# A windowed attention and gMLP kernel on one core: a new order of all steps, other engines for copies, and another choice of gMLP steps in 64-column halves

## The chip, the core and the metric

The kernel runs on one core of a Trainium2 chip. A core has five engines, each with its own queue of instructions that it takes strictly in order: TensorE (PE, matrix products), VectorE (DVE), ScalarE (ACT), GpSimd (POOL) and SyncE (SP, which issues nearly all DMAs here; its steps are marked DQ). Engines wait for one another by semaphores. The metric is device time of one execution in microseconds (us); lower is better.

## What is computed

Sliding-window attention (8 batches, 8 heads, 576 positions, head size 64, window 64), then a gMLP layer with a spatial gate over its output:

```python
scores = scale * np.matmul(q, k.transpose(0, 1, 3, 2))
mask = (rel >= 0) & (rel < window)
scores = np.where(mask, scores, -1000000000.0)
attn = np.exp(scores - max); attn = attn / (sum(attn) + 1e-09)
x = attn @ v                                # to (batch, 576, 512)
h = np.maximum(x @ w_in, 0.0)               # 512 -> 1024
u, v = h[..., :512], h[..., 512:]
v_n = (v - mu) / np.sqrt(var + 1e-06)
v_s = np.einsum('ts,bsd->btd', w_spatial, v_n) + b_spatial[None, :, None]
out = (u * v_s) @ w_out                     # 512 -> 512
```

## The kernel before

The program is 1113 steps. Each is a small function that emits the instructions of one piece of work for one engine. A step's name gives its kind, batch and part. Lines are those of kernel.py.

Loading, for batch b and group g of four heads (`load_steps`, line 419): `ldq`, `ldk` (line 424, 128x1152 f32 each) and five `ldv` (line 445, 128 rows of v each, the last 64; cut in packets of 256 bytes) are DMAs. `cq`, `ck` cast to f16; `tq`, `tk` (line 431) transpose on DVE. `cv` casts v into `hv`; `sl`, `su` and `s4` copy it into `hs`, shifted by 64 rows. On POOL a cast of q or k is three instructions (`cp`, line 314), on ACT or DVE one. Which engine does a copy is not fixed in the function: the listed step says it.

Attention (`att_steps`, 478, and `rem_steps`, 547, for the last 64 queries, marked `_r`): S is the scores (64 small matmuls in tiles of 32 rows, line 490), E the exponential on ACT (497), M the mask as a minimum on DVE (500), Z the sums (513), N and n logarithm and exponential of minus it, so the inverse, on ACT (539, 541), P the product with v (524), X the scaled result on DVE (532).

gMLP (`gmlp_steps`, 669), per batch: V_0 to V_3 (679) and V_4 (691; it also does the last 64 output rows of the batch before, 694) give the v half; Vr (658, ACT) takes it out of PSUM, Vb and Va (660, 662, DVE) make mean and variance, L1 and L2 (ACT) the inverse deviation, A (717, DVE) the normalized rows. U_0 to U_4 and Ur (746, ACT) give the u half. G multiplies by the spatial matrix, Ge (776, DVE) gates. O and Oe (635, ACT) give the output, `st` stores it. At the start `ldwin`, `ldwsp`, `ldwo`, `ldb` load the weights in pieces, `cwin`, `cwsp`, `cwo`, `cb` cast them, and W0 to W4 with We0 to We4 transpose the spatial matrix. D steps are filler matmuls on a zero tile.

What sets the order: the string `ORDER` (line 18) lists every step with its engine and the buffer numbers that it takes. `as_listed` (183) reads it, and lines 828 to 836 emit the steps in that order. So each engine's queue is the list cut down to its steps, and a load waits in SP's queue until the earlier user of its buffer (`BUFS`, 150: 8 for q, k and weights, 4 for v) is done with it. PSUM has two pairs of banks for S and four single banks (0 to 3) for all other products; a product waits until the bank's earlier content has been taken out.

`halves` (606) emits a product of a gMLP step. A step in the set `HALVED` does each product as two matmuls with 64 columns of weights into the two halves of the partitions (line 611) instead of one with 128 columns (line 608). Z, P, V_4 and O7_4 always work in 64 columns, S always in 32-row tiles. Before, `halved(2)` (197) chooses by rule: a run of gMLP products goes in halves where 64-column steps stand on both sides of it, or on one side of a run of at most two; U0_0 to U0_4 are added. That gives 92 steps in halves.

Of the kernel before, what the change touches and what calls it, by code (L numbers as in the profile page):

```python
# [26 lines left out]
ldwin110:DQ:7 cv0_01:DVE N0_00:ACT:2 ldwin111:DQ su0_01:DVE sl0_01:POOL Z0_r:PE:2 su0_10:DVE
Z0_11:PE:3 ldwin101:DQ N0_r:ACT:3 D9:PE:0 s40_0:POOL tk1_0:DVE:5 n0_00:ACT ldb:DQ:1 D8:PE:1
ldk1_1:DQ:2 n0_10:ACT D13:PE:2 ldq1_1:DQ:3 n0_01:ACT P0_01:PE:0 cv0_11:DVE ldwin000:DQ:0 P0_00:PE:1
sl0_11:DVE su0_11:POOL N0_11:ACT:4 S1_0:PE:0:1 ldwin001:DQ X0_00:DVE:0 ldwin010:DQ:4 n0_11:ACT  # L30
cwin110:POOL D20:PE:2 s40_1:DVE ldwin011:DQ E1_00:ACT:1 D19:PE:3 cwin111:POOL X0_01:DVE P0_10:PE:1
ldwsp3:DQ:5 P0_11:PE:2 cwin101:POOL E1_01:ACT:0 X0_10:DVE:1 D18:PE:3 ldwsp2:DQ:7 D3:PE:0 X0_11:DVE
cwin100:ACT P0_r:PE:1 M1_00:DVE n0_r:ACT cb:ACT V0_1:PE:3 ldwsp1:DQ:6 M1_01:DVE ck1_1:POOL:2
V0_2:PE:0 X0_r:DVE:0 Vr0_1:ACT:0 ldwsp4:DQ:1 Z1_00:PE:2 Vb0_1:DVE:0 V0_0:PE:1 N1_00:ACT:5
ldv1_00:DQ:2 cq1_1:POOL:3 tk1_1:DVE:0 Vr0_2:ACT:1 V0_3:PE:3 Vr0_0:ACT:2 cwin000:ACT ldwsp0:DQ:2
n1_00:ACT Z1_01:PE:2 V0_4:PE:0 D25:PE:1 D26:PE:1 ldv1_01:DQ cwin010:POOL tq1_1:DVE:1 cwin001:ACT
N1_01:ACT:2 cwin011:POOL ldv1_02:DQ Vr0_3:ACT:3 Vb0_2:DVE:1 S1_1:PE:0:1 cwsp3:POOL ldv1_03:DQ
Vr0_4:ACT:4 Vb0_0:DVE:2 U0_2:PE:1 E1_11:ACT:2 cwsp2:POOL Vb0_3:DVE:3 U0_3:PE:2 Va0_2:DVE cwsp1:POOL
E1_10:ACT:3 Va0_3:DVE Va0_1:DVE Vb0_4:DVE:4 U0_4:PE:3 Va0_0:DVE Va0_4:DVE M1_11:DVE ldv1_04:DQ
L10:ACT:0 U0_1:PE:0 Ur0_3:ACT:0 M1_10:DVE ldk2_0:DQ:3 Ur0_2:ACT:1 S1_r:PE:1:0 ldv1_10:DQ:3 cwsp4:DVE  # L40
Z1_11:PE:2 L20:ACT Ur0_1:ACT:2 U0_0:PE:1 A0_4:DVE cwsp0:DVE E1_r0:ACT:1 ldv1_11:DQ E1_r1:ACT
A0_0:DVE:0 Ur0_4:ACT:3 W0:PE:0 A0_3:DVE:1 ldq2_0:DQ:0 N1_11:ACT:1 cv1_00:DVE:2 cv1_01:POOL W2:PE:3
ldv1_12:DQ M1_r:DVE Ur0_0:ACT:4 W3:PE:2 ldv1_13:DQ sl1_00:ACT:2 sl1_01:POOL W4:PE:1 We0:DVE
s41_0:ACT We2:DVE We3:ACT W1:PE:0 su1_01:POOL su1_00:DVE Z1_r:PE:3 We4:ACT ldv1_14:DQ ck2_0:POOL:0
A0_2:DVE:2 P1_01:PE:2 N1_r:ACT:0 P1_00:PE:1 ldk2_1:DQ:4 Z1_10:PE:3 A0_1:DVE:3 ldwo10:DQ:5 We1:DVE
N1_10:ACT:4 ldq2_1:DQ:7 X1_00:DVE:2 G0_4:PE:0 n1_01:ACT ldwo00:DQ:6 G0_3:PE:3 n1_10:ACT ldwo11:DQ
cv1_10:POOL:3 X1_01:DVE ldwo01:DQ tk2_0:DVE:2 sl1_10:ACT:3 su1_10:POOL G0_0:PE:1 cq2_0:ACT:1
ldq3_0:DQ:1 cv1_11:POOL ldv2_00:DQ:0 Ge0_3:DVE:0 s41_1:POOL G0_2:PE:2 sl1_11:ACT Ge0_4:DVE:1
su1_11:POOL n1_r:ACT tq2_0:DVE:3 n1_11:ACT ldk3_0:DQ:2 G0_1:PE:3 ck2_1:POOL:2 cwo10:ACT ldv2_01:DQ
Ge0_2:DVE:2 P1_10:PE:0 P1_11:PE:2 X1_10:DVE:3 S2_0:PE:1:0 X1_11:DVE cq2_1:POOL:3 ldv2_02:DQ  # L50
P1_r:PE:0 E2_00:ACT:0 Ge0_0:DVE:3 U1_2:PE:2 ldv2_03:DQ Ge0_1:DVE:4 E2_01:ACT:1 U1_1:PE:1 X1_r:DVE:1
M2_00:DVE Ur1_2:ACT:5 V1_3:PE:3 cwo01:POOL tk2_1:DVE:0 cwo11:ACT Ur1_1:ACT:0 cwo00:POOL V1_1:PE:0
Vr1_3:ACT:5 M2_01:DVE cq3_0:POOL:0 V1_2:PE:2 Vr1_1:ACT:6 ldv2_10:DQ:1 Vb1_3:DVE:5 V1_4:PE:1
ldv2_11:DQ tq2_1:DVE:1 Vr1_2:ACT:7 Z2_01:PE:3 Vr1_4:ACT:4 V1_0:PE:0 ck3_0:POOL:1 Vb1_2:DVE:1
N2_01:ACT:3 tq3_0:DVE:4 S2_1:PE:1:0 Oe0_4:ACT:0 ldv2_12:DQ Vr1_0:ACT:2 U1_0:PE:2 ldk3_1:DQ:3
cv2_00:POOL:1 Va1_2:DVE E2_11:ACT:3 Va1_3:DVE ldv2_13:DQ Vb1_1:DVE:3 Z2_00:PE:3 O0_2:PE:1 ldv2_14:DQ
Vb1_0:DVE:0 E2_10:ACT:2 Vb1_4:DVE:2 ldv2_04:DQ U1_4:PE:0 N2_00:ACT:5 Va1_1:DVE ldv3_10:DQ:2
S2_r:PE:0:1 Va1_0:DVE Va1_4:DVE tk3_0:DVE:5 L11:ACT:1 O0_0:PE:3 Oe0_2:ACT:0 ldq3_1:DQ:0 E2_r0:ACT:0
ldv3_11:DQ Ur1_4:ACT:3 M2_11:DVE U1_3:PE:1 L21:ACT ldv3_12:DQ E2_r1:ACT A1_4:DVE Oe0_0:ACT:1
O0_1:PE:0 A1_2:DVE:4 ldq4_0:DQ:4 Ur1_0:ACT:1 A1_3:DVE:5 ldv3_13:DQ A1_1:DVE:6 Ur1_3:ACT:4  # L60
S3_0:PE:0:1 A1_0:DVE:7 ldv5_10:DQ:3 n2_00:ACT M2_10:DVE Z2_11:PE:3 Oe0_1:ACT G1_0:PE:2 M2_r:DVE
sl2_00:ACT:0 su2_00:POOL Z2_r:PE:1 N2_11:ACT:2 G1_3:PE:0 Ge1_0:DVE:5 s42_0:ACT cv2_10:POOL:0
# [120 lines left out]
def as_listed(plan):  # L183

    by = {s.name: s for s in plan.steps}
    out = []
# [10 lines left out]
def halved(longest):  # L197
# [6 lines left out]
    for name in seq:  # L204
        if not runs or runs[-1][0] != kind(name):
            runs.append((kind(name), []))
# [660 lines left out]
```

## Time and profile before

| what | value |
|---|---|
| time, median of 3 runs | 199.65 us (199.64 to 199.7) |
| profiled execution, span from first to last instruction | 198.2 us |
| its own whole time | not listed; the median is 1.4 us over its span |
| PE busy | 187.3 us (94%), 3337 matmuls |
| ACT busy | 168.4 us (85%) |
| DVE busy | 158.4 us (80%) |
| POOL busy | 76.9 us (39%) |
| DMA moved | 42.74 MB, mean 216 GB/s |
| granted TensorE clock | 0.998 |

Busy time is the union of an engine's instructions; matmuls overlap, so PE's is no sum of its steps. Windows give the same numbers for a stretch of the span, with the share of time in which the 16 DMA engines had packets (it can exceed 1, as packets overlap). The chain of waits is followed back from the last instruction; its rows are start, length and what held the end up. "DMA to landing" is the time from a load's issue to the last of its packets.

### The profile page before, as it was taken

The page shows a single profiled execution, that of the slowest core. Times are in us where ns is not written, and L with a number is a line of the kernel's source. Part 1 is how long each engine was busy: PE and PEld are TensorE (multiplying, and loading weights), DVE is VectorE, ACT ScalarE, POOL GpSimd, SP SyncE. Part 2 cuts the span into 40 slices and gives each one's busy share as a digit, 9 for nine tenths or more (in the row PEclk, how much of TensorE's full clock was granted, in tenths as well). Part 3 has the DMA queues.
Part 4 walks back from the last instruction along what each step waited for, and adds up shares of the span by engine and source line. Part 5 has one row for each costly group of instructions (what it writes and reads, how often), then busy time and mean ns, then how long its engine had stood idle before and what let it go on. Part 6 is the DMA issues. An engine that isn't in the chain of part 4 may idle for free.

```text
span 198.2 us, 7839 instructions
## 1 busy us (share of the span) xinstructions
PE 187.3 (94%) x3337; PEld 109.7 (55%) x3337; DVE 158.4 (80%) x306; ACT 168.4 (85%) x305; POOL 76.9 (39%) x147
## 2 busy tenths in 40 slices
PE   7788999999999999989999999999999999999991
PEld 2333565666556665565476567466465565764450
DVE  4799999999796899869999798887958684757420
ACT  2589889878899999989999999999999999558341
POOL 5232584747776689121999299100000000000000
PEclk9999999999999999999999999999999999999999
DMA  6998999999689989989999993878721110500535
GB/s 221 384 289 178 383 365 222 308 366 372 140 203 286 343 239 255 276 195 266 322 253 235 262 294 83 251 205 228 235 107 65 49 41 5 215 0 0 179 115 187
DMA packets 50278, 42.74 MB, mean 216 GB/s; under 512 B 39361, under 2 KB 39489, under 8 KB 50242
## 3 DMA queue, kind: packets, MB, share of 16 engines
q1 hardware_dynamic: 50018, 41.91, 71.9%
q8 instruction: 26, 0.43, 0.9%
q10 hardware_dynamic: 224, 0.33, 0.5%
q14 instruction: 10, 0.08, 0.1%
HBM read 32.79 MB, written 9.44 MB: 213 GB/s over the span
## 4 chain that ended last, share of the span: by engine, by line
PE 42%; ACT 20%; DMA 20%; DVE 6%; SPq 5%; issue 3%; POOL 3%; POOLq 0%
PE bank L611 17%; PE bank L608 17%; DMA nv<-in_v_dram 9%; DMA nk<-in_k_dram 7%; SPq L445 4%; DMA ws<-in_moe_w_spatial_dram 4%; ACT e L497 3%; ACT ob L635 3%; ACT lz L539 3%; ACT hs L316 2%; ACT lz L541 2%; PE pair L490 2%; PE bank L524 2%; ACT ru L746 2%; ACT vs L658 2%
## 5 line engine op out<-in xcount | busy, mean ns | idle before, releaser
L497 ACT ACTIVATE e<-pair 128x1024 f16<-128x1024 f32 x32 | 31.8, 1024 | 2.8 <-PE pair L490 2.6
L611 PE MATMUL bank<-wspT,vn 128*64 128x512 f16 (+3 forms) x440 | 32.4, 296 | 0.3
L776 DVE TENSOR_TENSOR g<-bank,ru 128x512 f16<-128x512 f32 (+1 forms) x40 | 24.6, 629 | 9.1 <-PE bank L608 4.4
L660 DVE BATCH_NORM_STATS2 st<-vs 128x6 f32<-128x512 f16 (+1 forms) x40 | 25.7, 671 | 2.8 <-ACT vs L658 2.8
L658 ACT ACTIVATE vs<-bank 128x512 f16<-128x512 f32 (+1 forms) x40 | 23.0, 602 | 5.6 <-PE bank L611 3.2
L532 DVE TENSOR_TENSOR x<-bank,lz 128x512 f16<-128x512 f32 x32 | 21.4, 683 | 6.5 <-PE bank L524 5.0
L746 ACT ACTIVATE ru<-bank 128x512 f32<-128x512 f32 (+1 forms) x40 | 21.6, 562 | 4.5 <-PE bank L608 4.4
L635 ACT COPY ob<-bank 128x512 f32<-128x512 f32 (+1 forms) x39 | 22.8, 589 | 2.1 <-PE bank L608 1.9
L611 PEld LDWEIGHTS <-vn 128*64 128x64 f16 (+1 forms) x440 | 18.6, 110 | 10.7 <-issue 1.3
L319 POOL CAST hk<-nk 128x384 f16<-128x384 f32 x33 | 16.3, 530 | 19.3 <-DMA nk<-in_k_dram 18.9
L500 DVE TENSOR_TENSOR e<-e,mask 128x1024 f16<-128x1024 f16 x32 | 21.9, 701 | 1.2 <-ACT e L497 1.2
L611 PE MATMUL bank<-win,x 128*64 128x512 f16 x184 | 22.4, 379 | 0.0
L431 DVE STREAM_TRANSPOSE qT<-hq 128x576 f32<-128x576 f32 x16 | 19.8, 1240 | 3.2 <-POOL hq L319 3.0
L611 PE MATMUL bank<-x,win 128*64 128x512 f16 (+1 forms) x288 | 22.3, 298 | 0.0
L431 DVE STREAM_TRANSPOSE kT<-hk 128x576 f32<-128x576 f32 x16 | 19.9, 1246 | 0.7 <-POOL hk L319 0.4
L541 ACT ACTIVATE lz<-lz 128x512 f32<-128x512 f32 x32 | 19.7, 635 | 0.1
L539 ACT ACTIVATE lz<-bank 128x512 f32<-128x512 f32 x32 | 18.6, 606 | 1.2 <-PE bank L513 1.1
L717 DVE TENSOR_SCALAR vn<-vs,mv,ln 128x512 f16<-128x512 f16 (+1 forms) x40 | 15.8, 447 | 4.2 <-ACT ln L707 4.1
L319 POOL CAST hq<-nq 128x384 f16<-128x384 f32 x30 | 15.7, 559 | 7.4 <-DMA nq<-in_q_dram 6.4
L322 POOL COPY hs<-hv 64x512 f16<-64x512 f16 (+1 forms) x28 | 16.2, 607 | 4.4 <-issue 3.7
L816 PE MATMUL bank<-scratch 128*128 128x512 f16 (+1 forms) x68 | 15.6, 379 | 1.3 <-DVE scratch L257 1.3
L611 PE MATMUL bank<-wout,g 128*64 128x512 f16 x128 | 16.1, 380 | 0.0
(89 smaller groups left out, 333.0 us busy)
## 6 DMA issues: line engine op xcount, KB each, us to landing
nq<-in_q_dram SPq DMA_DIRECT2D x16, 576.0 KB, 6.0
nk<-in_k_dram SPq DMA_DIRECT2D x16, 576.0 KB, 5.8
nv<-in_v_dram SPq DMA_DIRECT2D x64, 128.0 KB, 5.2
out_dram<-ob SPq DMA_DIRECT2D x14, 512.0 KB, 4.7
wi<-in_moe_w_in_dram SPq DMA_DIRECT2D x8, 256.0 KB, 6.0
ws<-in_moe_w_spatial_dram SPq DMA_DIRECT2D x4, 288.0 KB, 7.0
nv<-in_v_dram SPq DMA_DIRECT2D x16, 64.0 KB, 4.8
wo<-in_moe_w_out_dram SPq DMA_DIRECT2D x4, 256.0 KB, 8.1
```

The lines of the kernel that those rows point to most:

```text
L319: nc.gpsimd.tensor_copy(o[:, n:n + 384], i[:, n:n + 384])
L431: d = add(f"t{name}{b}_{g}", ("DVE", 1.09), key, lambda e: nc.vector.transpose(qt.t[:, :].rearrange("p (i j) -> p j i", j=18), h.t[:, :].b ...
L497: ex = add(f"E{b}_{g}{u}", ("ACT", 0.91), key, lambda e, u=u: nc.scalar.activation(e2[u].t[:, :, :], sc[u].t[:, :, :], AF.Exp, bias=0.0, s ...
L539: a = add(f"N{tag}", ("ACT", 0.06 + 0.00083 * n), key, lambda e: nc.scalar.activation(lz.t[:, 0:n], zb.t[:, 0:n], AF.Ln), deps=[z], acq=[l ...
L541: c = add(f"n{tag}", ("ACT", 0.09 + 0.00083 * n), key, lambda e: nc.scalar.activation(lz.t[:, 0:n], lz.t[:, 0:n], AF.Exp, bias=0.0, scale= ...
L608: nc.tensor.matmul(o[:, :], w, x, start=start, stop=stop)
L611: nc.tensor.matmul(o[c:c + 64, :], w[:, c:c + 64], x, start=start, stop=stop)
L635: lambda e: (nc.vector.tensor_copy if last else nc.scalar.copy)(view(), m.t[rows, 0:n]),
L658: rl = add(f"Vr{b}_{j}", ("ACT", 0.49), key, lambda e: nc.scalar.activation(vs.t[0:jn, :], m.t[0:jn, :], AF.Relu), deps=[pv], acq=[vs], us ...
L660: s1 = add(f"Vb{b}_{j}", ("DVE", 0.6), key + 0.02, lambda e: nc.vector.bn_stats(st6.t[0:jn, 0:6], vs.t[0:jn, :]), deps=[rl], acq=[st6], us ...
L746: lambda e, m=m, ru=ru, n=n: nc.scalar.activation(ru.t[:, 0:n], m.t[:, 0:n], AF.Relu), deps=[pu], acq=[ru], uses=[m])))
L776: lambda e, m=m, g=g, ru=ru, n=n: nc.vector.tensor_tensor(g.t[:, 0:n], m.t[:, 0:n], ru.t[:, 0:n], ALU.mult),
```

## The change

The string `ORDER` is new from its first to its last step. It holds the same 1113 steps with the same DMAs; `BUFS` and all step functions are as before. On every engine, SP among them, the steps stand in another order and take other buffer numbers. 62 copies have another engine: 31 go from ACT to POOL, 12 from DVE to POOL, 8 from POOL to ACT, 7 from POOL to DVE, 3 from DVE to ACT, 1 from ACT to DVE. That makes 285 steps on ACT (306 before, two of them stores in both), 285 on DVE (292) and 99 on POOL (71).

The rule `halved` is gone. A gMLP step in halves is marked PH in the list in place of PE, and `as_listed` reads PH as PE; there are 111. 35 steps are halved that were not, 16 are no more (among them V0_0 to V0_3, U0_0 to U0_3, G0_0 and G0_3).

Of the list, the diff below keeps some of the old order around batch 1, the new order from the load of v for batch 0 to S2_1, the line with `cq5_1`, and both ends.

```diff
 ORDER = """
...
-ldv1_12:DQ M1_r:DVE Ur0_0:ACT:4 W3:PE:2 ldv1_13:DQ sl1_00:ACT:2 sl1_01:POOL W4:PE:1 We0:DVE
-s41_0:ACT We2:DVE We3:ACT W1:PE:0 su1_01:POOL su1_00:DVE Z1_r:PE:3 We4:ACT ldv1_14:DQ ck2_0:POOL:0
-A0_2:DVE:2 P1_01:PE:2 N1_r:ACT:0 P1_00:PE:1 ldk2_1:DQ:4 Z1_10:PE:3 A0_1:DVE:3 ldwo10:DQ:5 We1:DVE
-N1_10:ACT:4 ldq2_1:DQ:7 X1_00:DVE:2 G0_4:PE:0 n1_01:ACT ldwo00:DQ:6 G0_3:PE:3 n1_10:ACT ldwo11:DQ
-cv1_10:POOL:3 X1_01:DVE ldwo01:DQ tk2_0:DVE:2 sl1_10:ACT:3 su1_10:POOL G0_0:PE:1 cq2_0:ACT:1
-ldq3_0:DQ:1 cv1_11:POOL ldv2_00:DQ:0 Ge0_3:DVE:0 s41_1:POOL G0_2:PE:2 sl1_11:ACT Ge0_4:DVE:1
-su1_11:POOL n1_r:ACT tq2_0:DVE:3 n1_11:ACT ldk3_0:DQ:2 G0_1:PE:3 ck2_1:POOL:2 cwo10:ACT ldv2_01:DQ
-Ge0_2:DVE:2 P1_10:PE:0 P1_11:PE:2 X1_10:DVE:3 S2_0:PE:1:0 X1_11:DVE cq2_1:POOL:3 ldv2_02:DQ
...
-G7_0:PE:0 U7_1:PE:1 Ge7_0:DVE:5 Ge7_3:DVE:6 G7_1:PE:3 Ur7_1:ACT:1 U7_4:PE:0 Ge7_1:DVE:7 G7_4:PE:2
-Ur7_4:ACT:5 O7_2:PE:1 Ge7_4:DVE:9 O7_0:PE:3 Oe7_2:ACT:1 st7_2:DQ O7_1:PE:0 Oe7_0:ACT:0 st7_0:DQ
-O7_3:PE:2 Oe7_1:ACT st7_1:DQ O7_4:PE:1 Oe7_3:ACT st7_3:ACT Oe7_4:DVE:0 st7_41:ACT st7_40:DQ
...
+s40_0:POOL E0_r0:ACT:0 E0_r1:ACT ldwin100:DQ:6 tq1_0:DVE:4 su0_10:POOL D9:PE:1 ldk1_0:DQ:7 D7:PE:0
+ldv0_12:DQ su0_01:POOL ck1_0:DVE:2 cwin100:ACT D24:PE:1 D19:PE:0 M0_r:DVE Z0_r:PE:1 N0_01:ACT:1
+n0_01:ACT P0_01:PE:3 D11:PE:0 ldv0_13:DQ cv0_11:POOL sl0_11:POOL M0_11:DVE Z0_11:PE:0 N0_00:ACT:2
+n0_00:ACT ldv0_14:DQ s40_1:POOL ldwin111:DQ n0_10:ACT su0_11:POOL ldwin101:DQ ldq1_1:DQ:0
+tk1_0:DVE:5 N0_r:ACT:3 cq1_1:POOL:3 ldwin000:DQ:1 cwin000:POOL ldwin010:DQ:2 cwin010:POOL
+N0_11:ACT:4 ldk1_1:DQ:3 n0_11:ACT P0_00:PE:2 ldwsp4:DQ:5 cwin101:ACT cwin111:ACT P0_r:PE:1
+ldwin001:DQ P0_10:PE:0 X0_00:DVE:0 cwsp4:POOL ldwin011:DQ ldv1_10:DQ:2 cwin001:POOL cwin011:POOL
+P0_11:PE:2 S1_0:PE:1:0 X0_01:DVE ldv1_11:DQ cv1_10:POOL:2 X0_10:DVE:1 X0_11:DVE D1:PE:3
+sl1_10:POOL:2 E1_00:ACT:0 V0_0:PE:0 Vr0_0:ACT:0 E1_01:ACT:1 su1_10:POOL tq1_1:DVE:0 ldwsp1:DQ:7
+ldb:DQ:6 V0_1:PE:3 n0_r:ACT M1_00:DVE V0_2:PE:2 Vr0_2:ACT:1 ck1_1:DVE:1 V0_3:PE:0 X0_r:DVE:0
+tk1_1:DVE:1 ldv1_12:DQ ldv1_13:DQ Vr0_1:ACT:2 Vb0_0:DVE:0 Va0_0:DVE Vb0_2:DVE:1 Vr0_3:ACT:3
+Z1_00:PE:1 ldwsp3:DQ:4 Vb0_1:DVE:2 N1_00:ACT:5 cb:POOL V0_4:PE:2 Vr0_4:ACT:4 S1_1:PE:1:0 E1_10:ACT:2
+E1_11:ACT:3 ldwsp0:DQ:0 U0_0:PE:3 Ur0_0:ACT:0 U0_4:PH:0 Vb0_3:DVE:3 Va0_1:DVE Vb0_4:DVE:4 ldv1_14:DQ
+Va0_2:DVE cv1_11:POOL Ur0_4:ACT:1 D22:PE:1 ldwsp2:DQ:5 S1_r:PE:1:0 cwsp3:ACT cwsp1:DVE U0_1:PE:2
+ldk2_0:DQ:3 Va0_4:DVE ldq2_0:DQ:1 ldk2_1:DQ:2 ldv1_00:DQ:3 sl1_11:POOL cwsp0:POOL Va0_3:DVE
+ldv1_01:DQ ldv1_02:DQ M1_11:DVE U0_2:PE:1 L10:ACT:0 L20:ACT D12:PE:3 Z1_11:PE:0 su1_11:POOL
+M1_10:DVE E1_r0:ACT:1 E1_r1:ACT ldv1_03:DQ ldv1_04:DQ cwsp2:DVE s41_1:POOL Ur0_1:ACT:2 ck2_0:POOL:0
+ldq2_1:DQ:6 A0_4:DVE ldwo10:DQ:7 Ur0_2:ACT:3 cq2_0:POOL:2 ldq3_0:DQ:4 M1_r:DVE W1:PE:3 ldwo11:DQ
+We1:ACT W2:PE:2 Z1_10:PE:1 A0_2:DVE:0 A0_1:DVE:1 N1_11:ACT:2 ldv2_10:DQ:1 W0:PE:3 ldv2_11:DQ
+Z1_r:PE:0 N1_10:ACT:1 A0_3:DVE:2 N1_r:ACT:0 We0:ACT W4:PE:1 n1_10:ACT M1_01:DVE We4:ACT We2:DVE
+ldwo00:DQ:0 ldwo01:DQ ck2_1:POOL:3 ldv2_12:DQ U0_3:PE:2 W3:PE:0 We3:ACT P1_10:PE:3 ldv2_13:DQ
+Z1_01:PE:1 A0_0:DVE:3 ldv2_14:DQ ldk3_0:DQ:5 ldq3_1:DQ:3 ldv2_00:DQ:0 tk2_0:DVE:2 n1_11:ACT
+P1_11:PE:0 Ur0_3:ACT:4 tq2_0:DVE:3 S2_0:PE:1:0 X1_10:DVE:2 tk2_1:DVE:0 cv1_00:POOL:3 sl1_00:POOL:3
+su1_00:POOL N1_01:ACT:4 cv1_01:DVE su1_01:POOL E2_01:ACT:2 X1_11:DVE G0_3:PE:3 sl1_01:ACT
+Ge0_3:DVE:0 G0_0:PE:2 s41_0:ACT n1_00:ACT Ge0_0:DVE:1 P1_00:PE:1 ldv3_10:DQ:2 X1_00:DVE:3 n1_r:ACT
+E2_00:ACT:3 P1_r:PE:0 ldk3_1:DQ:1 X1_r:DVE:1 cq2_1:POOL:1 G0_2:PH:3 tq2_1:DVE:1 P1_01:PE:2 n1_01:ACT
+cq3_0:ACT:0 X1_01:DVE G0_4:PE:1 Ge0_4:DVE:2 U1_4:PE:0 Ur1_4:ACT:5 cwo00:POOL cwo11:ACT tq3_0:DVE:4
+S2_1:PE:0:1 E2_10:ACT:0 E2_11:ACT:1 U1_3:PH:2 cwo10:ACT cv2_10:POOL:1 V1_2:PH:0 Vr1_2:ACT:5
...
+G1_0:PH:1 ldq5_1:DQ:4 cq5_1:ACT:2 su3_10:POOL V2_3:PH:0 Vr2_3:ACT:2 Ge1_0:DVE:8 ldv4_00:DQ:1
...
+Ge7_0:DVE:1 G7_1:PE:0 Ge7_1:DVE:0 G7_2:PE:1 G7_4:PE:3 Oe6_3:ACT st6_1:DQ Ge7_2:DVE:5 O7_0:PE:2
+Oe7_0:ACT:1 st7_0:DQ O7_1:PE:0 Oe7_1:ACT O7_2:PE:1 Oe7_2:ACT:0 U7_4:PE:2 Ur7_4:ACT:5 O7_3:PE:0
+Ge7_4:DVE:7 O7_4:PE:1 Oe7_3:ACT Oe7_4:DVE:0 st7_1:DQ st7_2:DQ st7_3:ACT st7_41:ACT st7_40:DQ
 """
...
@@ -186,7 +186,7 @@
     out = []
     for word in ORDER.split():
         name, eng, *banks = word.split(":")
-        out.append((by.pop(name), eng, [int(x) for x in banks]))
+        out.append((by.pop(name), "PE" if eng == "PH" else eng, [int(x) for x in banks]))
     assert not by, sorted(by)[:5]
     return out
 
@@ -194,27 +194,7 @@
 CHOOSE = as_listed
 
 
-def halved(longest):
-
-    def kind(name):
-        return "s" if name[0] == "S" else "v" if name[0] in "ZP" or (
-            name[0] == "V" and name.endswith("_4")) else "f"
-    seq = [w.split(":")[0] for w in ORDER.split() if w.split(":")[1] == "PE" and w[0] != "D"]
-    runs = []
-    for name in seq:
-        if not runs or runs[-1][0] != kind(name):
-            runs.append((kind(name), []))
-        runs[-1][1].append(name)
-    out = set()
-    for a, (what, names), c in zip([("f", [])] + runs, runs, runs[1:] + [("f", [])]):
-        near = (a[0] == "v") + (c[0] == "v")
-        if what == "f" and not any(n[0] == "W" for n in names) and (
-                near == 2 or near == 1 and len(names) <= longest):
-            out.update(names)
-    return out
-
-
-HALVED = halved(2) | {f"U0_{i}" for i in range(5)}
+HALVED = {w.split(":")[0] for w in ORDER.split() if w.split(":")[1] == "PH"}
 
 
 @with_exitstack
```

## The prediction

> **What bounds the kernel now.** I read the page first, then busy time by windows, then TensorE's timeline, then the waits.
>
> From the page:
>
> ```profile
> PE 187.3 (94%) x3337; PEld 109.7 (55%) x3337; DVE 158.4 (80%) x306; ACT 168.4 (85%) x305; POOL 76.9 (39%) x147
> ...
> PE   7788999999999999989999999999999999999991
> ...
> ACT  2589889878899999989999999999999999558341
> ```
>
> TensorE (PE) is full from about 25 us to the end, ACT nearly full to about 170. From the windows (us, then busy PE, PEld, DVE, ACT, POOL, clock, DMA share, GB/s):
>
> ```profile
> 15.00:20.00 5.00, 4.13 (x69) 1.81 (x68) 4.80 (x11) 4.64 (x11) 1.06 (x2) 1.00 0.80 179
> ...
> 30.00:35.00 5.00, 5.00 (x121) 2.75 (x107) 5.00 (x15) 5.00 (x13) 2.20 (x3) 1.00 1.18 235
> ...
> 150.00:160.00 10.00, 10.00 (x150) 5.26 (x150) 8.19 (x14) 9.89 (x17) 0.00 (x0) 1.00 0.15 56
> ```
>
> There are two stages: until about 60 us the DMA engines are full too (share 1.18) and DVE has no idle time; late, DMA and POOL do nothing and ACT is at 99%. A busy PE hides short waits, so I priced PE by the starts of its steps (its instruction counts per step match the list exactly, so each can be found in the trace):
>
> ```profile
> 94.35 1.24 PE L608 MATMUL bank<-wspT,vn 128*128 128x512 f16 x5
> 95.43 1.03 PE L608 MATMUL bank<-win,x 128*128 128x512 f16 x4
> 96.29 1.03 PE L608 MATMUL bank<-x,win 128*128 128x512 f16 x4
> 97.16 1.24 PE L608 MATMUL bank<-wspT,vn 128*128 128x512 f16 x5
> 98.24 1.03 PE L608 MATMUL bank<-x,win 128*128 128x512 f16 x4
> 99.20 0.68 PE L490 MATMUL pair<-qT,kT 32*128 32x64 f16 x64
> ```
>
> From start to start a V, U or O step takes 0.863 (95.43 to 96.29), G 1.083, and the step ahead of a differently shaped one 0.96 (98.24 to 99.20): a change of tile shape costs 0.097. In halves V, U, O and G take the same 0.863 and 1.083; only U_4 (0.503 against 0.466) and G_4 (0.632 against 0.601) grow. Z takes 0.216, P 0.250, S 0.613, W 0.46.
>
> Over its list from the first V step (23.59) to the end of O7_4 (194.06), 170.5 us, these sum to 161.5 and its changes of shape (28 at 0.097, 16 behind an S step at 0.024) to 3.1, together 164.7. So 5.8 us are waits: 1.9 before S2_1 (52.67) and 3.9 behind it. The tail, to 198.2, is 4.1. The median of the runs is 199.65, 1.4 over this span; I add 1.4 to every span below.
>
> **The change, part by part.** No step, transfer or buffer goes. *Halves.* 111 steps against 92: 89 matmuls more. The 512-column ones are priced at 0 by the rows above; one U_4 more is in halves, 0.04. *Order on PE.* Costly changes of shape from the first V step: 34 against 28, +0.58; three fillers of 0.43 instead of two of 0.55, +0.2. The sum becomes 165.5, 0.8 us more.
>
> The Trainium skill, TensorEngine Tiling (Array Packing), Restrictions, says that column tiling disables fast weight loads. The trace has 110 ns for a 64-column load and 98 ns for a 128-column one, hidden: steps take 0.863 either way. By that rule with loads in the open, 89 x 0.110 would add 9.8 us; by the rows nothing.
>
> *Engines of copies.* 62 copies move; ACT gives 32 (27.1 us by their rows: a cast of 1152 columns 1.15, shifts 0.83 and 1.04) and takes 11 (8.8), a net 18 us. POOL's steps sum to 98 us against 73. As PE has 165 us to do behind the first V step and POOL then 87, POOL's work is hidden beside it, with 10 us and more ahead of P and S from batch 3 on. For ACT, 18 us are off the path save where a late ACT now holds PE: the chain of waits has ACT work end just ahead of P3_00, G2_3, G4_3 and G6_4, which come 0.24 to 0.32 late, 1.1 together. The longest late gap, 0.93 inside S4_1, is none of these: the chain says "issue" there, 1.8 us after an instruction fetch at 85.4, and PE waited for no data. From the chain (start, length, what):
>
> ```profile
> 82.34 0.59 ACT ob L635
> 82.94 0.51 ACT lz L539
> 83.49 2.99 PE bank L611 x56
> ...
> 87.14 0.75 issue
> ```
>
>
> *Start.* What precedes the first V step is the same set of steps and loads, so that step is moved by the v chain. Loads land one after another. The trace's spacings: q or k 1.54, 128 rows of v 0.56, a piece of w_in 0.68, of w_spatial 0.72; the first lands at 4.6, so the sum starts at 3.1. Sums run ahead of the trace: k2_0 has 33.3 and landed at 37.65. The lag grew by 0.9, 1.1, 0.7 and 0.4 around the 16 KB instruction fetches at 12.9, 22.3, 28.5 and 33.5 (1.0 to 1.3 us on one of the 16 engines; a load waits for all) and by 0.9 in the window of share 0.80. After: v0_13 sums to 18.5, +0.9 is 19.4. POOL then does cv0_11, sl0_11, s40_1, su0_11 (0.67, 0.64, 0.46, 0.67), 21.9. P0_10 22.0, P0_11, S1_0, filler, V0_0 at 23.65. Before: 23.59. Ends: 22.7 without lag, 24.3 at before's pace.
>
> *To S2_1, the deciding stretch.* The new list puts S2_0 at 15.03 us of PE work behind V0_0 (before 20.08), S2_1 at 20.89 (27.20), but their loads hardly earlier. Ahead of and with q2_0: 10 q/k (15.4), v (7.6), w_in (5.4), w_spatial and bias (3.3), 34.9 with 3.1. Lag: the four fetches, 3.1, without the gap of 0.9, as fewer v loads come in a row: 38.0. Then cq2_0 on POOL (rows 1.4 to 1.8, ACT 1.15), 39.5, and DVE: cwsp2 (its load 34.9) 35.4, five A steps, M1_r, M1_01, We2 2.9, tk2_0, tq2_0 1.09 each, 40.75. S2_0 at 40.8, where PE alone would stand at 38.7: 2.1 of waiting. PE comes through W to the same point: W needs cwsp2, W1 35.45, then 4.8 and 0.4 of chains of evictions, 40.65. q2_1 is 5.6 us of loads behind q2_0 and sums to 40.5; one more fetch and what it did at 41.6 (1.4) make 45.0. cq2_1 46.5, tq2_1 47.65, S2_1 47.75. PE alone: 40.8 + 5.85 = 46.65. So 1.1 more. Ends for S2_1: 43.5 with no lag, 49 with before's lag of 5.6.
>
> The Trainium skill, GPSIMD Engine Reference, Specifications, says that GpSimd shares its SBUF interfaces with VectorE and contends with two-input instructions. The trace shows POOL casts spread (cq2_1 took 1.77 where others take 1.36). By the slow one S2_1 would come 0.3 later than in my sum.
>
> *Behind S2_1.* PE has 144.6 us left (before 137.5, as it had done 7.1 more by then, at 52.67). So at S2_1 the new kernel is 4.9 us earlier with 7.1 more to do: 2.2 behind. Waits: before's 3.9, less 0.9 of the 1.1 that ACT causes (next late there are the DVE steps that read the same banks, so I leave 0.2), plus 0.2, as U7_4 now stands before O7_3 and its Ur and Ge (0.38 and 0.42) end 0.2 too late for O7_4: 3.2. The gap of 0.93 stays in: there are more instructions to fetch, not fewer. End of PE: 47.75 + 144.6 + 3.2 = 195.55; tail 4.1, span 199.65; time **201.0**.
>
> The unknown is these waits; nothing in a trace of another order shows them. Bounds: 0.9 (O7_4's 0.2, and 0.5 where Ge0_1 ends after PE wants its bank for U1_0, and little else) and 5 (as now, with DVE full until 64). I take 3.2, near the only row, before's 3.9.
>
> **The rivals.** *Faster, 198.8.* ACT's relief takes nearly all late waits: 0.9 instead of 3.2, 2.3 less. For it: ACT at 9.9 of 10 in 120 to 170. Against: PE is at 9.9 to 10.0 there too. It decides when fewer than 1.7 us of wait are left behind S2_1. Chance 0.23. *No difference, 199.8.* The change does not do what it says: POOL takes 18 us off ACT, but no PE step was late for them, and the earlier place of S2_1 gives nothing, as its wait grows by as much; S2_1 then comes at 46.5, a fetch falling between loads, and 1.2 of the loss goes. 0.12. *ACT held by loads, 202.8.* cq5_1 goes to ACT, ahead of Vr2_3, whose bank U2_4 waits for. q5_1 sums to 62.4; with before's lag of 9.2 there it lands at 71.6, the cast and Vr2_3 end at 73.5, PE is there at 71.7: 1.8 more than forecast. For it, ACT's waits for a load now (4.1 us in one case); against, the freer DMA queue. 0.14. *Loads of weights in the open* by the rule of the Trainium skill's TensorEngine Tiling page; as a mechanism here 89 x 0.110 of the row, 210.8; the trace speaks against it. 0.01. **My forecast**, slower by 0.2 to 1.2%, 200.1 to 202: 0.50.
>
> **How the numbers follow.** What a measurement can tell from no change is 0.2%, 0.4 us. Slower 0.50 + 0.14 + 0.01 = 0.65, same 0.12, faster 0.23. The range leaves out about 0.1 on each side. Its lower edge, 198.2, is S2_1 at 47.2 with the low bound of waits (47.2 + 144.6 + 0.9 + 4.1 + 1.4); its upper edge, 203.4, is S2_1 at 48.8 with 4.5 of waits.
>
> **What would show it.** V0_0 near 23.6; S2_0 and S2_1 near 40.8 and 47.7, with q2_0 and q2_1 landing at 38.0 and 45.0 and DVE's transposes as what ended their waits; about 3 us of PE waits behind; ACT's busy time near 150; halved steps at 0.863 and 1.083. I am wrong if S2_1 starts before 46.5, or if all PE waits behind S2_1 fall under 1.7 us; then it is faster.

## The result, and the profile after

The kernel after takes 208.68 us (median of 6 runs, 206.82 to 210.16) beside 199.64 us before. The ratio, 1.043 (95% interval 1.0375 to 1.0486), is of the runs within 1.5% of the fastest of their kernel, and leaves out the profiled execution of the kernel after (210.05 us, span 208.3, mean clock 0.981 where the run of 206.82 us has 0.990), whose numbers so stand at the upper end. The forecast was 201.0 us, 198.2 to 203.4. The sign was right; the loss, 9.0 us, is more than six times the forecast one, and the time lies outside the range.

From the page of that execution: busy time by engine, three rows of 40 slices, the granted clock, and one row of the DMA queues (packets, MB, share):

```profile
PE 189.8 (91%) x3426; PEld 114.0 (55%) x3426; DVE 163.5 (78%) x299; ACT 155.1 (74%) x284; POOL 109.3 (52%) x193
...
PE   7678599988999998979996999999999999999991
...
ACT  3369739989989898978993889996989667634531
...
PEclk9999969999999999999997999999999999999998
...
q8 instruction: 27, 0.44, 0.9%
```

ScalarE is relieved (155 us busy, 168 before), GpSimd took the work (109 us busy, where its steps were priced at 98), TensorE has the 89 matmuls more. But TensorE's row has holes where before had nines, and the clock row has a 6 and a 7 in the middle, where before it was at nine from end to end. The same two rows from the page before:

```profile
PEclk9999999999999999999999999999999999999999
...
q8 instruction: 26, 0.43, 0.9%
```

Windows of 3.41 us of the kernel after, around the two places (columns as in the prediction; the third number from the end is the granted clock):

```profile
22.82:26.23 3.41, 1.41 (x101) 1.25 (x102) 3.08 (x5) 2.48 (x4) 2.84 (x6) 1.00 1.03 323
26.23:29.64 3.41, 3.31 (x9) 1.16 (x9) 1.53 (x3) 0.39 (x1) 1.90 (x4) 0.50 1.03 251
108.14:111.56 3.42, 0.90 (x68) 0.74 (x65) 3.17 (x9) 1.40 (x3) 3.04 (x4) 1.00 1.17 293
111.56:114.98 3.42, 3.42 (x69) 1.73 (x55) 0.94 (x2) 1.61 (x2) 1.42 (x2) 0.50 0.56 195
```

In the first and third TensorE is busy for 1.41 and 0.90 us only; in the window behind each the clock is 0.50. The list of TensorE's waits (in total, times, longest) says what it waited for:

```profile
PE pair L470 <- issue: 4.2, 2, 2.5
...
PE bank L504 <- issue: 1.1, 1, 1.1
PE bank L573 <- POOL hs L304: 1.0, 1, 1.0
PE pair L470 <- DVE g L756: 0.7, 1, 0.7
```

"issue" is time in which the engine waited for nothing that the profile shows: no data, no buffer. Its timeline (start, length, what; idle before it):

```profile
23.99 0.69 PE L470 MATMUL pair<-qT,kT 32*128 32x64 f16 x63
26.33 0.20 PE L470 MATMUL pair<-qT,kT 32*128 32x64 f16 x1 [1.66 <-issue]
...
108.60 0.26 PE L470 MATMUL pair<-qT,kT 32*128 32x64 f16 x9
111.38 0.82 PE L470 MATMUL pair<-qT,kT 32*128 32x64 f16 x55 [2.52 <-issue]
112.13 1.49 PE L591 MATMUL bank<-wout,g 128*64 128x512 f16 x6
```

S1_0 stops with 63 of its 64 matmuls done, S5_1 with 9: both in the middle of a step whose inputs were all there, as its first matmuls had run. (I call such a stop a standstill.) What can still be missing is instructions. The row "q8 instruction" is the fetch of them: 27 packets of 16 KB. A matmul and its weight load are two instructions, so TensorE's 6852 make some 27 blocks of 256. I counted TensorE's instructions up to each packet and each standstill of the trace (weight loads, matmuls, and the two to four DRAIN and EVENT_SEMAPHORE instructions in its queue):

| packet | starts | TensorE stopped at instruction | gap in TensorE's starts | it goes on | behind the packet's start |
|---|---|---|---|---|---|
| 2 | 23.68 | 2 x 256 + 193 | 1.85 | 26.33 | 2.66 |
| 5 | 48.67 | 5 x 256 + 193 | 0.79 | 51.34 | 2.67 |
| 6 | 55.55 | 6 x 256 + 193 | 0.79 | 58.09 | 2.54 |
| 11 | 87.51 | 11 x 256 + 193 | 1.26 | 89.98 | 2.47 |
| 14 | 108.81 | 14 x 256 + 193 | 2.71 | 111.38 | 2.57 |

All five stop at the same place of a block, with 193 of its instructions done. (The profile lays the second, S2_1, to Ge0_4, the last DVE step to end before it; S2_1 needs tq2_1, which had ended at 50.44.) The one row of "issue" in the kernel before is the same: packet 12 at 85.38, stopped at 12 x 256 + 193, 0.94 us, on again 2.52 behind the packet. A packet seems to be asked for about 283 instructions ahead of that place: in the twelve traces of this document none starts more than 0.12 us before the instruction at 256n - 90. In the kernel after, packets behind 118 us, where few loads are left, start 0.6 to 1.7 us after it (one 2.9, in the stretch from 130 to 140 us with a DMA share of 0.76); ahead of that, while the loads run, 1.1 to 5.5 us after it (mean 3.3). So TensorE has about 6 us for 283 instructions while loads run. A V step in halves has 16 in 0.86 us; an S step has 128 in 0.61, a P step 32 in 0.25. If the 283 fall on dense steps, TensorE runs dry.

That gave the first theory (**instruction supply**): the new order and the new halves shift and crowd the stream so that block ends fall on S and P steps while the DMA engines are full of loads; the half clock comes on top. Rivals: the **order itself** (late data, GpSimd's chain at the start), the **engines of the copies**, the **halved steps**, and two S steps **too close**, wherever the blocks end.

### The profile page after: what moved, and what is told of

Read it like the earlier page. It is cut to its first block, busy times and chain, and to the rows that moved or that the text cites. A ratio compares the mean times of both kernels' runs of the same rounds, so it can differ in the third digit from the quotient of the medians.

```text
span 208.3 us, 8060 instructions
## 1 busy us (share of the span) xinstructions
PE 189.8 (91%) x3426; PEld 114.0 (55%) x3426; DVE 163.5 (78%) x299; ACT 155.1 (74%) x284; POOL 109.3 (52%) x193
## 4 chain that ended last, share of the span: by engine, by line
PE 72%; DVE 9%; SPq 6%; issue 5%; DMA 4%; ACT 1%; POOL 1%; DVEq 0%; POOLq 0%; ACTq 0%
PE bank L591 43%; PE bank L588 12%; PE pair L470 4%; DMA nv<-in_v_dram 4%; PE bank L504 3%; PE bank L671 3%; SPq L425 3%; PE bank L493 3%; DVE e L480 2%; DVE x L512 2%; SPq L330 2%; DVE g L756 2%; SPq L404 1%; PE bank L796 1%; DVE kT L411 1%
## 5 line engine op out<-in xcount | busy, mean ns | idle before, releaser
L591 PE MATMUL bank<-wspT,vn 128*64 128x512 f16 (+3 forms) x450 | 34.9, 298 | 0.5 <-issue 0.4
L638 ACT ACTIVATE vs<-bank 128x512 f16<-128x512 f32 (+1 forms) x40 | 23.2, 599 | 10.0 <-PE bank L674 4.2
L302 POOL COPY hs<-hv 64x512 f16<-64x512 f16 (+1 forms) x46 | 28.7, 655 | 1.1
L591 PE MATMUL bank<-x,win 128*64 128x512 f16 (+1 forms) x360 | 29.3, 298 | 0.0
L299 POOL CAST hk<-nk 128x384 f16<-128x384 f32 x33 | 20.6, 659 | 12.6 <-issue 7.7
L591 PE MATMUL bank<-win,x 128*64 128x512 f16 x216 | 26.7, 379 | 0.0
L299 POOL CAST hq<-nq 128x384 f16<-128x384 f32 x39 | 19.8, 542 | 13.1 <-DMA nq<-in_q_dram 7.8
L591 PE MATMUL bank<-wout,g 128*64 128x512 f16 x192 | 25.3, 397 | 0.0
L480 DVE TENSOR_TENSOR e<-e,mask 128x1024 f16<-128x1024 f16 x32 | 24.0, 769 | 0.8 <-ACT e L477 0.6
L697 DVE TENSOR_SCALAR vn<-vs,mv,ln 128x512 f16<-128x512 f16 (+1 forms) x40 | 18.2, 500 | 5.5 <-ACT ln L687 5.4
L591 PEld LDWEIGHTS <-win 128*64 128x64 f16 x360 | 15.7, 111 | 8.3 <-issue 0.6
```

The source lines that it names most:

```text
L299: nc.gpsimd.tensor_copy(o[:, n:n + 384], i[:, n:n + 384])
L302: nc.gpsimd.tensor_copy(o[:, lo:hi, :, :], i[:, lo:hi, :, :])
L480: mins.append(add(f"M{b}_{g}{u}", ("DVE", 0.65), key, lambda e, u=u: nc.vector.tensor_tensor(e2[u].t[:, :, :], e2[u].t[:, :, :], mask[:, : ...
L591: nc.tensor.matmul(o[c:c + 64, :], w[:, c:c + 64], x, start=start, stop=stop)
L638: rl = add(f"Vr{b}_{j}", ("ACT", 0.49), key, lambda e: nc.scalar.activation(vs.t[0:jn, :], m.t[0:jn, :], AF.Relu), deps=[pv], acq=[vs], us ...
```

## The experiments

For the supply theory I made a sum: the times of TensorE's instructions from a trace, its standstills taken out; packet n starts 3.4 us behind instruction 256n - 90 (1.0 behind 118 us), instruction 256n + 193 can start 2.55 us later. It gives 8.4 us of standstill for the kernel after (measured 7.2 over the steps' own time) and 0.5 for the kernel before. By single packets it is less exact, since it takes one delay for all: it has over 1 us at packet 9, where the trace has none, and nothing at packet 6, which cost 0.79. That the totals agree is in part luck.

**1. The same kernel, its blocks shifted.** Fillers on a zero tile are cut finer, nothing else:

```diff
+CUT = {21: 8, 2: 8, 23: 8, 0: 8, 15: 8, 17: 8, 14: 4}
-            for c in range(2 if i < NWARM - NFILL else FILL):
-                n = 512 if i < NWARM - NFILL else 128
+            for c in range(CUT.get(i, 2) if i < NWARM - NFILL else FILL):
+                n = 1024 // CUT.get(i, 2) if i < NWARM - NFILL else 128
```

> The kernel after, with seven of the clock-raising filler steps that stand ahead of S0_0 cut finer (six of them into 8 matmuls of 128 columns, one into 4 of 256, in place of 2 of 512). They stream the same 1024 columns each; nothing else is touched, but every later instruction of TensorE stands 76 places (38 matmuls with their 38 weight loads) further back in its stream. Theory 1, the instruction supply: the DMA page of the profile after has a queue q8 named instruction, 27 packets of 16 KB, one for each 256 instructions of TensorE. In all five places where TensorE stood on no data (24.5, 50.6, 57.3, 88.7, 108.7 us; 1.85, 0.79, 0.79, 1.26 and 2.71 us) it had run to the same place, 193 instructions past a multiple of 256, and went on 2.5 to 2.7 us behind the start of that block's packet. With the blocks shifted by 76 instructions, the times of the trace after and a packet that starts 3.4 us behind the 90th instruction before each multiple of 256 give standstills of 2.8 us in all (0.7 to 7.9 for a packet at 2.5 to 4.3 us) where the same sum gives 8.5 without the shift: 201 to 204.5 us, no standstill over 1.5 us, at most one window of half clock. Theory 2, the order itself (data that come late, buffers, engines of copies): the shift changes nothing, 206.8 to 210 us.

Measured: 204.65 us (203.43 to 206.23), 1.0257 of before (1.0188 to 1.0327). That is 0.15 over the range of the first theory, and 2.2 under that of the second. 4.0 us of the 9 are gone for 38 more matmuls (3.5 by the ratios, 1.043 and 1.026, each taken beside its own runs of the kernel before). In its profile one standstill is left (0.78 us, packet 6, again at place 193), and the clock row holds nine throughout:

```profile
PEclk9999999999999999999999999999999999999999
```

The order, the engines, the halves and all data are those of the kernel after: where the block ends fall made these 4 us.

**2. The kernel before, shifted.** `CUT` with 8 for D14, D12, D23, D15, D22, D6, D0, D16, D21, D7, D11, D24 and D5.

> The kernel before, untouched but for 13 of its first filler steps, cut into 8 matmuls of 128 columns each in place of 2 of 512: the same columns, and all that follows stands 156 places further back in TensorE's stream of instructions. Theory 1, the instruction supply: by the same sum on the times of the trace before, the shift puts the ends of the blocks onto the dense steps: standstills near 33.5, 64.6, 87.6 (3.0 us), 103.5 and 108.2 us, 7.6 us in all (2.7 to 14.7) in place of 0.6, and a window of half clock where one of them passes 2 us: 204 to 210 us, as slow as the kernel after. Theory 2, the order itself: 199.3 to 200 us.

Measured: 205.29 us (204.11 to 206.41), 1.0304 of before (1.0248 to 1.0359): a mere change of fillers makes the good order nearly as slow as the new one. The time is in the first theory's range; the place was missed. The largest standstill is at the first packet, which my sum had not shown since it put the whole shift at time 0 (with the cuts at their own times it gives 2.2 us there):

```profile
12.12 0.67 PE L486 MATMUL pair<-qT,kT 32*128 32x64 f16 x63 [0.70 <-DVE qT L427]
15.52 0.21 PE L486 MATMUL pair<-qT,kT 32*128 32x64 f16 x1 [2.72 <-issue]
```

It is S0_1, stopped at 256 + 193, on again 2.75 us behind the packet; half clock follows for 3.41 us. At 87 us of the trace before (91.8 here), where I expected 3.0, packet 13 came early and only 0.36 was lost. When a packet starts is known to some 1.5 us, no better, and each start shifts what comes behind it.

**3. The engines of the copies put back.** The 62 words of the list get their old engine, in their new places (cq0_0 from ACT to POOL, and so on).

> The kernel after with the 62 copies that changed their engine put back on the engine they had in the kernel before, each at its place in the list of the kernel after; order and halved steps as in the kernel after. Theory 1, the instruction supply: TensorE's stream is the same instruction for instruction, so it runs dry in the same places: 205 to 210 us. Theory 3, the engines of copies (GpSimd's chain cv0_11, sl0_11, s40_1, su0_11, which V0_0 and P0_r wait for in the kernel after, goes to VectorE; ScalarE gets 30 copies back): if these cost the time, V0_0 starts near 24 us in place of 27.3 and the time is under 204 us.

Measured: 225.82 us (225.59 to 228.16), 1.134 of before. Both expectations missed the size: V0_0 comes at 31.15, S0_0 waits 5.6 us for its transpose in place of 1.6, as ck0_0 now stands behind ck0_1 on ScalarE, and ScalarE is late again in many places behind 120 us. The new engines belong to the new order. What it tells for the question: S5_1 stops at 14 x 256 + 193 as before, for 2.73 us, with all copies elsewhere and 6 us later in time.

**4. Two S steps moved.**

```diff
-P0_00:PE:2 ... P0_r:PE:1 ... P0_10 ... P0_11:PE:2 S1_0:PE:1:0
+P0_00:PE:2 ... S1_0:PE:1:0 P0_r:PE:1 ... P0_10 ... P0_11:PE:2
-P4_11:PE:0 S5_1:PE:1:0 E5_10:ACT:3 ... O2_1 ... O2_3 ... V4_3:PH:2
+P4_11:PE:0 ... O2_1 ... O2_3 ... V4_3:PH:2 S5_1:PE:1:0 E5_10:ACT:3
```

> The kernel after with two steps moved on TensorE: S1_0 from behind P0_11 to ahead of P0_r (into P0_r's wait of 1.2 us), and S5_1 with its exponential E5_10 from ahead of O2_1 to behind O2_1, O2_3 and V4_3, some 2.6 us later. Theory 1, the instruction supply as a budget: what counts is how many instructions stand between two places of the stream, not which step is the dense one. The block's packet starts when it did, S1_0's 128 instructions are used up earlier, and the six steps ahead of O2_1 alone reach the end of the block at 108.7 us: standstills of 2 to 2.7 us stay at both places (in P0_11 or the filler behind it, and in O2_1), and the time stays at 205 to 210 us. Theory 4, two dense steps too close (S5_0 and S5_1 stand 3.2 us apart in the kernel after, 8.8 in the kernel before; S1_0 behind five P steps): both standstills and both windows of half clock go, about 7 us: 200 to 203 us.

Measured: 207.95 us (206.93 to 210.79), 1.0401 of before. The timeline (S1_0 ran undisturbed at 22.07; the rows are the end of P0_11 and O2_3; lines of edited kernels differ by a few):

```profile
23.64 0.20 PE L500 MATMUL bank<-e,hv 128*64 128x64 f16 x1
26.36 0.21 PE L500 MATMUL bank<-e,hv 128*64 128x64 f16 x1 [2.52 <-issue]
...
110.19 1.02 PE L587 MATMUL bank<-wout,g 128*64 128x512 f16 x7 [0.21 <-issue]
```

The first half is as the budget says: the standstill left the S step and came in the last matmul of P0_11, 2.7 us, with its half clock. The second was wrong by size: the standstill moved into O2_3, but packet 14 started at 107.41 (2.6 behind its place, not 3.6) and only 0.59 was lost. "Too close" falls with the first half; neither theory had the second right.

**5. The loads of v first at the start, on top of 1.** `ldv0_12`, `ldv0_13`, `ldv0_14` moved from behind `ldk1_0` to behind `ldv0_04`.

> The kernel after with the fillers cut as in after_shift76, and with the loads v0_12, v0_13 and v0_14 put ahead of win100 and k1_0 on SyncE's list, right behind v0_04. In after_shift76 the first V step starts at 25.45 us, where the forecast had 23.65; P0_r stands 1.23 us for the last of GpSimd's four copies behind v0_13 (landed near 20.6, forecast 19.4). If that landing is what is left of the miss at the start, v0_13 lands about 2 us earlier (832 KB of win100 and k1_0 no longer ahead of it), P0_r's wait goes, and V0_0 starts near 24.2 us: 0.8 to 1.5 us less than after_shift76, 203 to 204 us in the median. If k1_0, which now lands some 1 us later, takes its place (S1_0 waits for its transpose), the time is that of after_shift76, 204.65 us, within 0.5.

Measured: 205.84 us (203.77 to 206.18), 1.0303 (1.0234 to 1.0371): not faster. GpSimd's chain ended at 20.97 in place of 23.2, but V0_0 started at 27.61. VectorE's timeline:

```profile
21.56 0.76 DVE L300 CAST hk<-nk 128x1152 f16<-128x1152 f32 x1 [2.13 <-DMA nk<-in_k_dram]
22.23 0.42 DVE L547 TENSOR_TENSOR er<-er,maskr 128x512 f16<-128x512 f16 x1
```

ck1_0 stands 2.13 us for the later load of k, and behind it in VectorE's queue wait M0_r and M0_11, which Z0_r and Z0_11 need: the second of the two cases on record, but dearer, since I had looked only at S1_0. TensorE stands 2.81 us ahead of Z0_r, and the window behind it, 23.79 to 27.20, is at half clock, which holds V0_0 back further. So the start is bound by both chains. The 205.84 itself says little of the start: the trace has 2.26 us of standstill at 5 x 256 + 193 and a second window of half clock behind it.

**6. Fewer bytes to load.**

```diff
...
+VH = [4, 4, 4, 1, 1, 1, 1, 1]
-                n.t[:, :], src[b, 4 * g:4 * g + 4, :, :].rearrange(...)
+                n.t[:, 1152 - 288 * VH[b]:1152], src[...].rearrange(...)[:, 1152 - 288 * VH[b]:1152]
-                nv.t[0:sn, c, :, :], v[b, 4 * g:4 * g + 4, ...]
+                nv.t[0:sn, c, 0:VH[b], :], v[b, 4 * g:4 * g + VH[b], ...]
...
```

Not shown: the buffers of the loads are made once and kept, so that what an earlier load left stays in them.

> The kernel after, with the loads of q, k and v of batches 3 to 7 cut to a quarter of their bytes (the rest of each buffer keeps what an earlier load left, so the numbers that those batches compute with are stale); order, engines, halved steps and every instruction of TensorE stay. Theory 1 in its second half says that the instruction packets come late since they queue behind loads: where the DMA engines are busy they start 3.4 us behind the 90th instruction ahead of a multiple of 256 (1.0 us where the engines are idle). From about 65 us on the packets should start 1 to 2 us behind it, and the standstills at 88.7 and 108.7 us (1.26 and 2.71 us) and the window of half clock behind the second should go; those before 60 us (1.85, 0.79, 0.79) stay: 201.5 to 204.5 us. If the place in the stream alone decides, whatever the loads do, both late standstills stay and the time is 206 to 210 us; so it is, too, if late loads of q, k, v were what TensorE stood on, with the difference that data waits would then go from the list of waits.

Measured: 204.28 us (203.19 to 206.12), 1.0256 (1.0182 to 1.033). Packets 9 to 15 start 0.6 to 1.8 us behind their places (1.1 to 4.8 in the kernel after). The standstills of packets 11 and 14 are gone, and so is that of 6; those of 2 and 5 (2.42 and 0.93 us) stay. S5_1 at the same place of the same stream, and the step behind it:

```profile
106.88 0.68 PE L477 MATMUL pair<-qT,kT 32*128 32x64 f16 x64
107.49 1.70 PE L598 MATMUL bank<-wout,g 128*64 128x512 f16 x14
```

So the place in the stream alone does not decide: the fetch is late where the full loads run. That it queues behind them is the likely reading, not shown by itself. Whether bytes or the number of packets counts is not told apart by this.

**7 and 8. The halves exchanged**, by name, in each order (words PE and PH of the list; in the kernel before a set in place of the rule).

> The kernel before with the 111 halved steps of the kernel after (by name) in place of its own 92; order and engines as in the kernel before. Changes of the tile shape: 81 in place of 63, at 0.097 us 1.7 us more. TensorE's stream is 170 instructions longer, bit by bit, so the ends of its blocks move. By the sum on the times of the trace before, standstills of 3.3 us (1.7 to 6.5), chiefly one of 1.3 to 2.5 near 88 us, in place of 0.5. Theory 1: 203 to 206 us, of which 1.7 the shapes. If halved steps cost by themselves (their weight loads in the open), steps of 0.863 and 1.083 us become longer and the time passes 207; if neither counts, 201.3.

Measured: 202.19 us (201.75 to 203.2), 1.0149 (1.0095 to 1.0202), 0.8 less than the low end on record. TensorE ends at 195.82, 1.74 later than in the profile before, with 0.60 us of standstill (at 89 us) in place of 0.94. Of the 1.74, 0.80 is there at the first V step already (24.39 and 23.59); the other 0.94 and the 0.34 less of standstill make 1.3 us, beside 17 changes of shape behind that step, priced at 1.65. The range failed by the supply: 3.3 us of standstill worked out, 0.60 found. The time is under the 207 of weight loads in the open, and does not tell the other two cases apart.

> The kernel after with the 92 halved steps of the kernel before (by name) in place of its own 111. Changes of the tile shape: 126 in place of 70, at 0.097 us 5.4 us more. The stream of TensorE is shorter by 178 instructions by its end; by the sum on the times of the trace after, standstills of 10.2 us (6.6 to 13.9) in place of 8.4: the one at 24.5 stays (2.0), the largest moves from 108.7 to about 49 us (2.9 to 4.1). Theory 1: 212 to 218 us. If the extra halved steps are what slowed the kernel after, this one is faster than it, under 206 us.

Measured: 220.54 us (215.54 to 222.08, profiled 222.08); the shortest run alone is inside the range on record, and the median is over it. The largest standstill moved where the sum had put it, to S2_1, by the sum at about 49 us of the trace after, which is packet 6:

```profile
51.89 0.57 PE L466 MATMUL pair<-qT,kT 32*128 32x64 f16 x50
56.46 0.40 PE L466 MATMUL pair<-qT,kT 32*128 32x64 f16 x14 [4.00 <-issue]
```

4.19 us at 6 x 256 + 193 (2.9 to 4.1 on record), and two windows of half clock. Fewer halved steps, a slower kernel: taking the extra halves out does not give the time back. How much they would cost by themselves this run does not tell, since it has 56 changes of shape more, priced at 5.4 us.

**9 and 10. Both kernels with their block ends set on sparse steps.**

> The kernel after with its order, engines and buffers, and with the ends of TensorE's blocks of 256 instructions put where the work is sparse: 16 of the fillers are cut finer (128 instructions more), eight whole steps (V0_0 to V0_3, U0_0, G0_0, G0_3, U1_4) are halved and ten halved ones (G1_4, G2_3, G3_0, U2_2, U2_3, U2_4, U3_2, U3_3, U4_1, V2_2) made whole, for 6 changes of the tile shape more (0.6 us). The sum on the times of the trace after, with packets 3.0, 3.6 and 4.2 us behind the 90th instruction ahead of a multiple of 256, gives standstills of 0, 0.5 and 1.3 us, where it gives 6.7, 9.5 and 13.3 without the edit. Theory 1: the time comes down from 208.7 to what the forecast had without standstills, with V0_0 near 25.4 us (as in after_shift76) in place of 23.65: 201.0 + 1.8 + 0.6 = 203.4 us, 201.5 to 204 us, no window of half clock behind the first 6 us. If what is left of the loss over after_shift76 is in the order, it is no faster than that, 204.65 us.

Measured: 204.54 us (203.10 to 207.04), 1.0256 (1.0219 to 1.0293). The profiled run, 203.1 us, is as worked out: V0_0 at 25.16, no half clock, one standstill of 0.79 in S2_1. TensorE ends at 197.66, 3.6 behind the kernel before, as much as the forecast's 1.5, 1.5 more at the start and 0.6 for the shapes make; since 0.75 of it is that standstill, the other waits are as much under the forecast. The median is over the range, which no trace explains. It is no faster than the kernel of 1.

> The kernel before, with the same treatment: ten fillers cut finer (72 instructions more), three whole steps halved (O0_0, O0_1, U1_3) and eight halved ones made whole (U1_1, U1_2, U1_4, U2_0, U2_2, V1_1, V1_3, V2_2), 5 changes of the tile shape more (0.5 us). In the trace before one standstill of 0.94 us is left to gain (at 87.0 us), and its single runs reach from 198.6 to 202.3 us. Theory 1: 198.4 to 199.8 us, and less spread upward; faster than before by more than 0.5 us only if most runs of it hold such a standstill. If the supply plays no part in the kernel before, 200.0 us (the 5 changes).

Measured: 201.23 us (199.46 to 204.39), 1.0073 (1.0042 to 1.0104): a miss (198.4 to 199.8 on record). Its profile has no standstill, and TensorE ends 1.5 us later than before all the same: it waits for data between 27 and 47 us (1.15 us ahead of U0_3 alone), where S2_0 comes 2.7 us later. Which load or copy began that I did not settle. No version here beats the kernel before.

## Why the prediction was wrong, point by point

The sign was right, and not by luck alone: with one short standstill left (experiment 9) TensorE still ends 3.6 us behind the kernel before, and 1.5 of that is what the forecast had. The size was wrong in two terms, the start and the waits behind S2_1. Both lacked the supply of instructions, and the start 1.5 us besides.

**Prices of steps: right.** From start to start a halved V or U step takes 0.86 in the kernel after, with twice the matmuls:

```profile
128.36 1.03 PE L591 MATMUL bank<-win,x 128*64 128x512 f16 x8
129.22 1.03 PE L591 MATMUL bank<-x,win 128*64 128x512 f16 x8
130.09 0.23 PE L504 MATMUL bank<-e,hv 128*64 128x64 f16 x4
```

The rival of weight loads in the open (the Trainium skill, TensorEngine Tiling (Array Packing), Restrictions) has nothing for it here. Yet pricing the 89 matmuls more at 0 was a price of time only. They are also 178 instructions, and no term of the sum had instructions in it.

**Start: the step from v0_13 at 19.4 over the chain to 21.9 to V0_0 at 23.65 failed.** V0_0 started at 27.30. v0_13 landed at 20.6, GpSimd's four copies took the 2.5 us priced and P0_r waited until 23.3; this and VectorE's products make 1.5 of it (without a standstill, in the kernel of experiment 9, V0_0 is at 25.16). VectorE, in the kernel after:

```profile
20.99 1.25 DVE L411 STREAM_TRANSPOSE kT<-hk 128x576 f32<-128x576 f32 x1
22.31 1.29 DVE L512 TENSOR_TENSOR x<-bank,lz 128x512 f16<-128x512 f32 x2
23.91 1.29 DVE L512 TENSOR_TENSOR x<-bank,lz 128x512 f16<-128x512 f32 x2 [0.32 <-PE bank L504]
```

The four X0 products that V0_0 reads end at 25.20, nearly back to back behind tk1_0: an earlier v0_13 would have won little, as experiment 5 shows. The other 2.2 are S1_0's standstill (1.77) and the filler behind it at half clock (0.39).

**V0_0 to S2_1: right in sum**, 24.04 us against 24.10, for mixed reasons: 0.79 of standstill and 1.16 of V0_0 and V0_1 at half clock lie in it, and less waiting for q2_0 and q2_1 than priced (q2_1 landed at 44.02, forecast 45.0). In the kernel of 9, without them, it is 23.94.

**Behind S2_1: the step of 3.2 us of waits, with bounds of 0.9 and 5, failed.** From S2_1 to the end of PE it is 152.7 us, not 147.8. In it: standstills of 0.57, 1.24 and 2.82, half clock behind the last 1.41, other waits 2.1. "The gap of 0.93 stays in" was the mistake in one phrase: I had seen the "issue" behind a fetch, and took for a constant what depends on where a block ends; I never asked where the 27 ends fall in the new stream. With little standstill the term holds: 148.56 in the kernel of 9, with 0.75 of standstill in it, against 147.8 and 0.6 for its six changes of shape. ACT's late waits went as forecast, and O7_4's 0.2 came.

The sum closes: start 3.65, middle -0.06, behind S2_1 4.9, together 8.5 us on the forecast end of PE (195.55; measured 204.04). With a tail of 4.3 (forecast 4.1) and 1.75 outside the span (1.4) that is the 210.05 of the profiled execution. Of the 8.5, supply and half clock make 10.2 (7.2 and 3.0); the start adds 1.5; of the waits that I had priced 3.2 are not there beside them, probably since data catch up while TensorE stands.

**Rivals.** None of the four had the mechanism, and they and the forecast had 0.99 of the chances under 203 us. The faster one falls (ACT's relief came, 155 us busy where 150 was forecast, and bought nothing), so does "ACT held by loads": no wait of V2_3 or U2_4 in the list.

**What stays open.** The other single runs of the kernels of 1 and 9 are 0.4 to 3.9 us longer than the profiled ones, with lower mean clocks (0.975 to 0.999 for 1.0); where their standstills fall is in no trace.

## What to carry to other kernels

Count instructions, not only time: where a page shows an instruction queue, find the place of a block at which it stops, and see how much time the new order gives from the request of a block to its use while loads run. Small matmuls packed closely (here 283 instructions in under some 6 us, an estimate from 3.4 and 2.55) were dear then, and shifting the stream by 76 or 156 instructions took 2% off one kernel and put 3% on the other; so shift the stream once by finer fillers before an order is judged by its time. A row of "issue" in the middle of a step is the sign.

## What the runs showed of the hardware that was not expected

- **The supply of instructions.** In 11 of the 12 traces TensorE stands for 0.5 us or more at an instruction 256n + 193, and goes on 2.3 to 3.1 us behind the start of a 16 KB packet. In none of the some 300 block crossings of these traces does it pass that place less than 2.2 us behind the packet. The Trainium skill, Runtime: NRT & Kernel Launch, Instruction fetch mechanics, says that an engine's instructions are refilled in blocks of 16 KiB, 256 instructions, by a DMA queue of the sequencer's own, and that the cost of crossing a block is mostly hidden. The block agrees with the 27 packets; "mostly hidden" holds in the kernel after behind 118 us (0 of 12 packets) and not while the loads run, where five packets cost 7.2 us. A dense stretch is enough by itself: in the kernel of experiment 8 packet 17 started 0.60 us behind its place, at 132.79, and TensorE still stood 1.20 us. The request comes some 283 instructions ahead, so TensorE has little more than one block in hand.
- **The half clock.** Over all windows of 3.41 us of the twelve traces (those in which a program's matmuls end left out), each of the twelve with 1.86 us or more of TensorE idle (up to 3.41) was followed by a window at 0.50; none with 1.81 or less was, if it was itself at full clock. The Trainium skill, TensorE: Matmul & The Clock Gate, Part 1, has the free-running window of 3413 ns, which agrees (the stretches at 0.50 last 3.41 or 6.83 us), but names a whole idle window as the limit; here a little over half a window was enough, and the idle time need not be in one piece (0.5 us for data and 1.5 for instructions in the window at 22.82).
- **Engines of copies are no free choice.** The old engines in the new order cost 17 us more than the new ones (225.8 and 208.7).
